# One product for values and denominators in an attention block followed by SwiGLU

## The chip, the cores and the metric

The kernel runs on one core of one Trainium2 chip. Its time is the device time of one execution in microseconds. Lower is better. The engines are named as in the profile: PE (matrix products), DVE (VectorE), ACT (ScalarE), POOL (GpSimd), SP (SyncE, which here only issues transfers).

## The reference

Attention over 4 batches, 8 heads, 768 positions and a head dimension of 64, with a mask and a bias, then a feed-forward block over the 3072 tokens of 512 features:

```
scores = q @ k.T / 8 - slope[h] * dist          # dist = 96 for far global keys
keep   = (key < 8) | (0 <= query - key < 96)    # 8 global keys, 96 local ones
a      = softmax(where(keep, scores, -1e9))
x      = a @ v                                   # to 3072 x 512
out    = (silu(x @ w_gate) * (x @ w_val)) @ w_out   # 512 -> 1536 -> 512
```

Inputs and the output are float32 in HBM.

## The kernel before

*Attention.* A batch has four pairs of heads (class `Pair`). Keys are cut into 7 chunks of 120, and each chunk is laid out with the 8 global keys in front, so that its 128 rows meet the 216 queries that can see it. Scores stand with keys on the partitions (`scores`, `scores_half`): the two heads of a pair use 64 rows of the array each. ACT takes the exponential into `at`, and DVE (POOL for some) multiplies it with a mask that holds the bias.

`values` (L386 to L439) forms one half of the queries (384) of one pair. With weights of 64 columns, head 0 writes partitions 0 to 63 and head 1 partitions 64 to 127: first a product with a tile of ones, which gives the denominator on all 64 partitions of a head (`den`), then a product with V (`num`). ACT copies the numerators to SBUF (`ns`, L419). DVE transposes the denominators in blocks of 32 by 32 (`dT`, L422), takes the reciprocal of 12 numbers a partition (`dR`, L423) and spreads it back by a second transpose (`rb`, L427). POOL, or DVE for batch 0, multiplies `ns` and `rb` into `xT` (L434), the input of the feed-forward part.

V stands in one tile for each batch, `vSs[b]`, of 128 x 7 chunks x 8 heads x 64 in float16. Its rows 8 and up are loaded by POOL, chunk by chunk (`load_v_rest`, L169), and its 8 global rows are copied from a small tile `vG` by SP (`copy_globals`, L183). POOL zeroes chunk 6 of batches 1 to 3 at the very start (L122); behind that in POOL's order stand the loads of v, and of k and q of heads 4 to 7, for the first half of batch 0, then weights, then the second half of k and q. For batch 0, V comes through a permutation by PE instead (`p_perm`, L547), with `v16` and `perm` as operands.

*Feed-forward.* Tokens go in 8 tiles of 384. For each tile and each of 12 column blocks f, `gate_or_val` makes a gate product and a value product of four matmuls each (`gps`, `vps`; L477), in a ring of three PSUM banks. ACT takes a tanh of the gate (`th`), and DVE makes `sl` (L490) and `hT` (L494) of it. `out_part` (L506) multiplies `hT` of the tile before with `wo`, three matmuls at a time. There are three buffers for `hT`.

*Order.* Everything stands in an order written out by hand. A prologue forms the first half of batch 0. Then seven stretches go through the tiles, and each has a list of attention steps that are strewn evenly between the feed-forward products (`stretches`, and the loop at L723; `quota` sets the spacing). The third stretch holds the first half of batch 1, the fourth (tiles 2 and 3) the second half of batch 1 and the first half of batch 2 (`both(1)`), the fifth (tiles 4 and 5) `both(2)`, the sixth (tile 6) the second half of batch 3. What a step leaves for DVE and POOL (masks, inversions, spreads, `spread_keys`) goes to a list `later`; one entry of it runs before each product, and all of it before the next step. Loads are tied to a tile and a block f by `at_step`. Keys and queries of batches 2 and 3 are transposed by DMA from SP (`transposes_dma`, L441), from rows that POOL loads. The lines that set the value steps and the V loads:

```python
        return [[sc(b, 0, 2), sc(b, 1, 2)], [sc(b, 2, 2), sc(b, 3, 2), fetch(0, 1)],
                [va(b, 0, 1), va(b, 1, 1)], [sp(0), va(b, 2, 1), va(b, 3, 1), sp(1)],
...
        items += [lambda b=b, c=c: load_v_rest(b, c) for c in range(NCH)]
```

The functions that the diff touches, with the line numbers of the profile:

Of the kernel before, what the change touches and what calls it, by code (L numbers as in the profile page):

```python
# [37 lines left out]
def kernel(  # L38
# [65 lines left out]
    k32 = sb2.tile([128, H // 2, J2 * D], FP32, name="k32", tag="kst")  # L104
    q16 = sb2.tile([128, 2, H, J2 * D], FP16, name="q16", tag="qst")
    k16 = sb2.tile([128, 2, H, J2 * D], FP16, name="k16", tag="kst")
    v16 = sb.tile([128, H, J2 * D], FP16, name="v16")
    for hp in range(2):
        for st, src in ((k32, k), (q32, q)):
            nc.sync.dma_start(  # L110
# [6 lines left out]
            out=dst, in_=src[0, h0:h1, TB * half:TB * half + TB, :].rearrange(  # L117
                "h (p j) d -> p h (j d)", p=128))

    vSs = [sb.tile([128, NCH, H, D], FP16, name=f"vS{b}") for b in range(B)]  # L120
    for b in range(1, B):
        nc.gpsimd.memset(vSs[b][:, 6, :, :], 0.0)  # L122
    load_half(v16, v, 0, 0, H)
    load_half(k16[:, 0, 4:8], k, 0, 4, 8)
    load_half(q16[:, 0, 4:8], q, 0, 4, 8)
# [3 lines left out]
    nc.vector.memset(ones, 1.0)  # L129

    NC0 = 4
    perm = sb.tile([128, J2, NC0, 128], FP16, name="perm")
    nc.vector.memset(perm.rearrange("p j c m -> p (j c m)").bitcast(mybir.dt.uint32), 0)
    kTs = [sb.tile([128, NCH * 128], FP16, name=f"kT{i}") for i in range(NP)]

# [33 lines left out]
    def load_v_rest(b, c):  # L169
        n = min(KC, S - KC * c)  # L170
        nc.gpsimd.dma_start(  # L171
            out=vSs[b][NG:NG + n, c, :, :],
            in_=v[b, :, KC * c:KC * c + n, :].rearrange("h p d -> p h d"))


# [5 lines left out]
            in_=v[:, :, 0:NG, :].rearrange("b h p d -> p (b h) d"))  # L181

    def copy_globals(b):  # L183
        c0 = 3 if b == 0 else 0
        nc.sync.dma_start(
            out=vSs[b][0:NG, c0:, :, :],
            in_=vG[:, b, :, :].unsqueeze(1).broadcast_to([NG, NCH - c0, H, D]))


    def stage_rows(b):  # L190
# [60 lines left out]
    class Pair:  # L251
# [134 lines left out]
        def values(self, half, nd, keep, mul_eng):  # L386
            b, hp = self.b, self.hp
            lo, hi_q = HALF[half]
            num, den = nd
            parts = []  # L390
            if b == 0:
                for which in range(2):
                    for c, col, q0, n in SCORES[half, which]:
                        parts.append((c, (half, which), col, q0 - lo, n))
            else:
                for c in range(NCH):
                    cb, col, q0, n = chunks[c]
                    a, z = max(q0, lo), min(q0 + n, hi_q)
                    if a < z:
                        parts.append((c, cb, col + a - q0, a - lo, z - a))  # L400
            for dst, ones_side in ((den, True), (num, False)):
                for i, (c, cb, col, o, n) in enumerate(parts):
                    vals = vS3 if (b, half, c) == (0, 0, 3) else vSs[b][:, c]
                    for hi in range(2):
                        r = slice(64 * hi, 64 * hi + 64)
                        nc.tensor.matmul(  # L406
                            dst[r, o:o + n],
                            lhsT=ones[:, 0:64] if ones_side else vals[:, 2 * hp + hi, :],
                            rhs=self.at[cb][:, hi, col:col + n],
                            start=(i == 0), stop=(i == len(parts) - 1),  # L410
                            skip_group_check=True)
            dT = sb2.tile([128, TB], FP32, name="dT", tag="dT")
            dR = sb2.tile([128, TB // 32], FP32, name="dR", tag="dR")
            rb = sb2.tile([128, TB], FP32, name="rb", tag="rb")
            dst = x_of(2 * b + half)[:, hp, :]
            src = num[:, 0:TB]
            if keep:
                src = sb2.tile([128, TB], FP32, name="ns", tag="ns")
                nc.scalar.copy(out=src, in_=num[:, 0:TB])  # L419

            def invert():
                nc.vector.transpose(dT, den[:, 0:TB])  # L422
                nc.vector.reciprocal(  # L423
                    out=dR, in_=dT.rearrange("p (n i) -> p n i", i=32)[:, :, 0])

            def spread():
                nc.vector.transpose(  # L427
                    rb.rearrange("p (n i) -> p n i", i=32),
                    dR.unsqueeze(2).broadcast_to([128, TB // 32, 32]))
                if mul_eng is nc.gpsimd:  # L430
                    scale_num()

            def scale_num():
                mul_eng.tensor_mul(dst, src, rb)  # L434

            later.append(invert)
            later.append(spread)
            if mul_eng is not nc.gpsimd:
                later.append(scale_num)  # L439

        def transposes_dma(self):  # L441
            b, hp = self.b, self.hp
# [23 lines left out]

    def products(t, f, which, c0, c1, dst=None):
        if f == 0 and which == 0 and c0 == 0:
            hTs[t] = sb2.tile([128, NFF, TB], FP16, name="hT", tag="hT", bufs=3)
        if c0 == 0:  # L470
            if dst is None:
                dst = single("gv"[which] + "ps", state["x"][gv.get("n", 0) % len(state["x"])])
                gv["n"] = gv.get("n", 0) + 1
            gv[f, which] = dst
        w = (wg, wv)[which]
        for c in range(c0, c1):
            nc.tensor.matmul(  # L477
                gv[f, which][:, 0:TB], lhsT=w[:, c, 128 * f:128 * f + 128],
                rhs=x_of(t)[:, c, :],
                start=(c == 0), stop=(c == NC - 1))  # L480
# [112 lines left out]
    for c in range(3, NCH):  # L593
        load_v_rest(0, c)
    load_w(3)
    for b in range(1, B):
        copy_globals(b)
    run_later(9)
    p_sc(2)
# [26 lines left out]

    def va(b, hp, half):
        def step():
            pairs[b, hp].values(half, banks("nd"), True,
                                nc.vector if b == 0 else nc.gpsimd)  # L630
        return step

    def tr(b, hp):
# [11 lines left out]
        return step  # L645

    def second(b):
        return [[sc(b, 0, 2), sc(b, 1, 2)], [sc(b, 2, 2), sc(b, 3, 2)],
                [va(b, 0, 1), va(b, 1, 1)], [va(b, 2, 1), va(b, 3, 1)]]

    def first(b):
        return [[tr(b, 0), tr(b, 1)],
# [5 lines left out]
    def both(b):  # L658
# [6 lines left out]
        def sp(hp):  # L665
            return lambda: later.append(pairs[n, hp].spread_keys)

        return [[sc(b, 0, 2), sc(b, 1, 2)], [sc(b, 2, 2), sc(b, 3, 2), fetch(0, 1)],
                [va(b, 0, 1), va(b, 1, 1)], [sp(0), va(b, 2, 1), va(b, 3, 1), sp(1)],
                [sc(n, 0, 0), sc(n, 0, 1), fetch(2, 3)], [sp(2), sc(n, 1, 0), sc(n, 1, 1)],  # L670
                [va(n, 0, 0), sc(n, 2, 0)], [sp(3), sc(n, 2, 1), va(n, 1, 0)],
                [sc(n, 3, 0), sc(n, 3, 1)], [va(n, 2, 0)], [va(n, 3, 0)]]

    half1 = [[trh(0)], [trh(1)], [sch(0, 0)], [sch(0, 1)], [trh(2)], [sch(1, 0)], [sch(1, 1)],
# [34 lines left out]
        at_step(0 if c < 2 else 1, (10 + c) % 12, lambda c=c: load_v_rest(1, c))  # L709
    for c in range(4, NCH):  # L710
        at_step(1, 2 * c - 1 if c < 6 else 10, lambda c=c: load_v_rest(1, c))
    for b, base, rate in ((2, 23, 2.0), (3, 43, 1.4)):
        items = [lambda b=b: stage_rows(b)]
        for hp in range(NP):
            for i in (1, 0):
                for hi in range(2):
                    items.append(lambda b=b, i=i, h=2 * hp + hi: load_rows(b, i, h))
        items += [lambda b=b, c=c: load_v_rest(b, c) for c in range(NCH)]
        for n, it in enumerate(items):
            at_step((base + int(n / rate)) // NFF, (base + int(n / rate)) % NFF, it)  # L720

    outs = [(t, i, part) for t in range(NT - 1) for i in range(3) for part in range(4)]
    for n, (tiles, steps) in enumerate(stretches):  # L723
# [3 lines left out]
                groups.append((0.05 if t == 0 and f < 2 else 1.0, t, f, which))  # L727
            groups += [(1.1, t, f, 2)] * n_out
        work = sum(g[0] for g in groups)
        quota = len(steps) / (work - (1.0, 0, 5.0, 3.0, 3.0, 4.5, 3.0)[n])  # L730
        owed = -0.1 if n == 0 else 0.4
        for w, t, f, which in groups:
            if which == 0:
# [55 lines left out]
```

## Time and profile before

| | |
|---|---|
| median of 9 runs | 263.65 us (263.19 to 264.51) |
| the profiled execution | 263.21 us, of which the span from first to last instruction is 261.2 |
| PE busy | 247.4 us, 95% of the span |
| DVE busy | 184.3 us, 71% |
| ACT busy | 134.6 us, 52% |
| POOL busy | 100.3 us, 38% |
| tile 0 begins, tile 2, tile 4, tile 6, tile 7 (first gate product) | 20.4, 82.1, 140.6, 197.7, 225.5 us |

A line of the timeline gives the start and the length in us, the engine, the line, what is written and read, how many instructions are merged, and in brackets the idle time before them and what ended it. A line of the chain gives start, length and what. A line of waits and groups gives busy time, mean duration and idle time. Matmuls overlap, so a run of them is longer than its share of PE by the latency of the last one.

### The profile page before, as it was taken

To read this page: it belongs to the slowest core of one execution; us is meant where nothing else is said; L and a number is where in the kernel's file an instruction comes from. 1 tells how busy PE (TensorE), PEld (TensorE's weight loads), DVE (VectorE), ACT (ScalarE), POOL (GpSimd) and SP (SyncE) were. 2 spreads that over 40 slices of the span, in tenths; PEclk is the share of its full clock that TensorE was granted. 3 is DMA by queue.
4 is the path that set the end of the run, shared out by engine and by line. 5 is a ranking of instruction groups with operands and counts; after the bars stand their busy time and mean duration, and the time that the engine had idled before them with its cause. 6 is when DMAs were issued, how large, how long until landed. Compare 5 with 4: busy or idle time off the path is not lost.

```text
span 261.2 us, 5568 instructions
## 1 busy us (share of the span) xinstructions
PE 247.4 (95%) x2144; PEld 140.5 (54%) x2144; DVE 184.3 (71%) x422; ACT 134.6 (52%) x296; POOL 100.3 (38%) x117
## 2 busy tenths in 40 slices
PE   7977999899999999899999999999999999999993
PEld 4554555465655566445555566455555565555541
DVE  7388689967787667987966668978876659655510
ACT  3565687469873554445633654555534633332321
POOL 9663653000237947901438886701111223300000
PEclk9999999999999999999999999999999999999999
DMA  7999999970354999991059996991011101101122
GB/s 167 184 192 167 189 204 203 193 47 4 52 71 61 121 143 133 176 141 36 9 71 89 141 172 65 134 140 42 2 40 44 40 3 40 40 3 40 40 83 80
DMA packets 81010, 24.82 MB, mean 95 GB/s; under 512 B 66832, under 2 KB 77912, under 8 KB 80984
## 3 DMA queue, kind: packets, MB, share of 16 engines
q0 software_dynamic: 63264, 13.83, 65.2%
q1 hardware_dynamic: 17720, 10.64, 18.3%
q8 instruction: 17, 0.28, 0.5%
q14 instruction: 9, 0.07, 0.1%
HBM read 28.63 MB, written 6.29 MB: 134 GB/s over the span
## 4 chain that ended last, share of the span: by engine, by line
PE 68%; DVE 13%; DMA 8%; ACT 4%; issue 3%; POOL 2%; POOLq 0%; DVEq 0%; ACTq 0%
PE ops L506 20%; PE vps L477 19%; PE gps L477 18%; DMA q<-in_q_dram 8%; PE nd L406 6%; PE sc L358 3%; DVE sl L490 3%; DVE hT L494 2%; DVE rb L427 2%; DVE dT L422 2%; ACT at L367 2%; PE trs L262 1%; ACT th L488 1%; DVE dR L423 1%; DVE xT L434 1%
## 5 line engine op out<-in xcount | busy, mean ns | idle before, releaser
L488 ACT ACTIVATE th<-gps 128x384 f32<-128x384 f32 x94 | 46.5, 494 | 67.1 <-PE gps L477 65.1
L490 DVE SCALAR_TENSOR_TENSOR sl<-th,gps 128x384 f32<-128x384 f32 x94 | 51.4, 547 | 40.0 <-ACT th L488 39.6
L477 PE MATMUL vps<-xT,wv 128*128 128x384 f16 x376 | 76.6, 326 | 2.0 <-DVE sl L490 1.6
L477 PE MATMUL gps<-xT,wg 128*128 128x384 f16 x376 | 77.0, 326 | 1.3 <-DVE hT L494 0.8
L506 PE MATMUL ops<-wo,hT 128*128 128x512 f16 x288 | 75.7, 380 | 0.0
L434 POOL TENSOR_TENSOR xT<-ns,rb 128x384 f16<-128x384 f32 x24 | 24.0, 999 | 96.0 <-DVE rb L427 92.0
L494 DVE TENSOR_TENSOR hT<-vps,sl 128x384 f16<-128x384 f32 x94 | 51.3, 546 | 6.9 <-PE vps L477 0.5
L477 PEld LDWEIGHTS <-wg 128*128 128x128 f16 x384 | 36.1, 98 | 34.7 <-issue 3.8
L477 PEld LDWEIGHTS <-wv 128*128 128x128 f16 x384 | 36.0, 98 | 28.5 <-issue 5.1
L506 PEld LDWEIGHTS <-hT 128*128 128x128 f16 x288 | 26.9, 98 | 24.9 <-issue 0.9
L367 ACT ACTIVATE at<-sc 128x432 f16<-128x432 f32 x72 | 33.0, 538 | 3.7 <-PE sc L358 3.7
L171 POOL DMA_DIRECT2D vS<-in_v_dram x25 | 22.1, 886 | 7.1 <-DMA wo<-in_moe_w_out_dram 4.9
L511 ACT ACTIVATE osb<-ops 128x512 f32<-128x512 f32 x24 | 14.4, 598 | 19.9 <-PE ops L506 19.9
L419 ACT COPY ns<-nd 128x384 f32<-128x384 f32 x28 | 13.4, 478 | 17.2 <-PE nd L406 16.4
L427 DVE STREAM_TRANSPOSE rb<-dR 128x384 f32<-128x384 f32 x32 | 18.1, 568 | 0.9
L378 DVE TENSOR_TENSOR at<-at,masks 128x864 f16<-128x864 f16 x20 | 14.4, 721 | 3.4 <-ACT at L367 3.2
L422 DVE STREAM_TRANSPOSE dT<-nd 128x384 f32<-128x384 f32 x28 | 16.0, 573 | 0.3 <-PE nd L406 0.3
L343 ACT ACTIVATE at<-sc 128x432 f16<-128x432 f32 (+2 forms) x32 | 11.9, 444 | 5.8 <-PE sc L335 5.8
L406 PEld LDWEIGHTS <-ones 128*64 128x64 f16 x288 | 10.9, 110 | 7.3 <-issue 6.8
L196 POOL DMA_DIRECT2D kst<-in_k_dram x16 | 13.7, 872 | 0.0
L196 POOL DMA_DIRECT2D qst<-in_q_dram x16 | 13.6, 865 | 0.0
L406 PE MATMUL nd<-at,ones 128*64 128x216 f16 (+6 forms) x256 | 13.2, 230 | 0.0
(77 smaller groups left out, 190.3 us busy)
## 6 DMA issues: line engine op xcount, KB each, us to landing
out_dram<-osb SPq DMA_DIRECT2D x24, 256.0 KB, 2.1
vS<-in_v_dram POOLq DMA_DIRECT2D x21, 120.0 KB, 6.6
wg<-in_moe_w_gate_dram POOLq DMA_DIRECT2D x6, 256.0 KB, 8.8
wv<-in_moe_w_val_dram POOLq DMA_DIRECT2D x6, 256.0 KB, 8.8
wo<-in_moe_w_out_dram POOLq DMA_DIRECT2D x3, 512.0 KB, 12.2
kst<-in_k_dram POOLq DMA_DIRECT2D x16, 96.0 KB, 4.4
qst<-in_q_dram POOLq DMA_DIRECT2D x16, 96.0 KB, 5.8
kst<-in_k_dram POOLq DMA_DIRECT2D x2, 384.0 KB, 14.9
```

The costliest lines, as they stand in the source:

```text
L171: nc.gpsimd.dma_start(out=vSs[b][NG:NG + n, c, :, :], in_=v[b, :, KC * c:KC * c + n, :].rearrange("h p d -> p h d"))
L196: nc.gpsimd.dma_start(out=st[:, h // 2, :, h % 2, :], in_=src[b, h].rearrange("(t p) d -> p t d", p=128))
L367: nc.scalar.activation(out=at[:, hi, :], in_=sc[hi][:, 0:BANK], func=AF.Exp, scale=scale)
L406: nc.tensor.matmul(dst[r, o:o + n], lhsT=ones[:, 0:64] if ones_side else vals[:, 2 * hp + hi, :], rhs=self.at[cb][:, hi, col:col + n], sta ...
L422: nc.vector.transpose(dT, den[:, 0:TB])
L427: nc.vector.transpose(rb.rearrange("p (n i) -> p n i", i=32), dR.unsqueeze(2).broadcast_to([128, TB // 32, 32]))
L434: mul_eng.tensor_mul(dst, src, rb)
L477: nc.tensor.matmul(gv[f, which][:, 0:TB], lhsT=w[:, c, 128 * f:128 * f + 128], rhs=x_of(t)[:, c, :], start=(c == 0), stop=(c == NC - 1))
L488: nc.scalar.activation(out=th, in_=dst[:, 0:TB], func=AF.Tanh, scale=0.5)
L490: nc.vector.scalar_tensor_tensor(out=sl, in0=th, scalar=1.0, in1=dst[:, 0:TB], op0=AluOp.add, op1=AluOp.mult)
L494: nc.vector.tensor_mul(hTs[t][:, f, :], dst[:, 0:TB], gv["sl"])
L506: nc.tensor.matmul(ops, lhsT=hTs[t][:, f, 128 * i:128 * i + 128], rhs=wo[:, f, :], start=(f == 0), stop=(f == NFF - 1))
```

## The change

Batches 1 to 3 get a V tile `vO` in which each head's 64 columns of V are followed by 64 columns of ones. Batches 1 and 3 share one. POOL writes the ones and the zeroes of chunk 6 at the start, for two tiles. Twenty value steps (second half of batch 1, all of batches 2 and 3) go through a new function, `values_full`: for each head by itself one product a chunk with 128 columns of weights, [V|1] for head 0 and [1|V] for head 1, into a PSUM bank of its own. So numerators and denominators of a head stand on opposite halves of the partitions. ACT copies each head's numerators, DVE inverts each head's denominators (two transposes of 64 partitions and two reciprocals in place of one of each), and the spread and POOL's product stay one. First halves of batches 0 and 1 and the second half of batch 0 keep `values`.

In the stretches each of these steps stands alone instead of in pairs, some change places with score steps, and the spacing changes. The V loads of batches 2 and 3 no longer follow the loads of k and q at their pace but have places and a pace of their own. The global rows are copied chunk by chunk for batches 1 and 2 (14 transfers), and for batch 3 in the middle of tile 4. `hT` gets two buffers instead of three, and `v16` and `perm` use one of them; `ns` gets four.

```diff
-    v16 = sb.tile([128, H, J2 * D], FP16, name="v16")
+    hT_pro = sb2.tile([128, NFF, TB], FP16, name="v16perm", tag="hT")
+    v16 = hT_pro[:, 0:4, :].rearrange("p f t -> p (f t)").rearrange("p (h e) -> p h e", h=H)
...
-    vSs = [sb.tile([128, NCH, H, D], FP16, name=f"vS{b}") for b in range(B)]
+    vSs = [sb.tile([128, NCH, H, D], FP16, name="vS0")]
+    vOs = [None]
     for b in range(1, B):
-        nc.gpsimd.memset(vSs[b][:, 6, :, :], 0.0)
+        if b < 3:
+            vOs.append(sb.tile([128, NCH, H, 2, D], FP16, name=f"vO{b}"))
+            nc.gpsimd.memset(vOs[b][:, :, :, 1, :], 1.0)
+            nc.gpsimd.memset(vOs[b][:, 6, :, 0, :], 0.0)
+        else:
+            vOs.append(vOs[b - 2])
+        vSs.append(vOs[b][:, :, :, 0, :])
     load_half(v16, v, 0, 0, H)
...
-        c0 = 3 if b == 0 else 0
-        nc.sync.dma_start(
-            out=vSs[b][0:NG, c0:, :, :],
-            in_=vG[:, b, :, :].unsqueeze(1).broadcast_to([NG, NCH - c0, H, D]))
+        if b == 0:
+            nc.sync.dma_start(
+                out=vSs[b][0:NG, 3:, :, :],
+                in_=vG[:, b, :, :].unsqueeze(1).broadcast_to([NG, NCH - 3, H, D]))
+        else:
+            for c in range(NCH):
+                nc.sync.dma_start(out=vSs[b][0:NG, c], in_=vG[:, b])
...
+        def values_full(self, half, pv):
...
+            rows = (slice(0, 64), slice(64, 128))
+            for hi in range(2):
+                for i, (c, cb, col, o, n) in enumerate(parts):
+                    w0 = 4 * D * hp + D * hi
+                    nc.tensor.matmul(
+                        pv[hi][:, o:o + n],
+                        lhsT=vOs[b][:, c].rearrange("p h s d -> p (h s d)")[:, w0:w0 + 2 * D],
+                        rhs=self.at[cb][:, hi, col:col + n],
+                        start=(i == 0), stop=(i == len(parts) - 1),
+                        skip_group_check=True)
+                nc.scalar.copy(out=ns[rows[hi], :], in_=pv[hi][rows[hi], 0:TB])
+
+            def invert(hi):
+                r = rows[1 - hi]
+                nc.vector.transpose(dT[r, :], pv[hi][r, 0:TB])
+                nc.vector.reciprocal(
+                    out=dR[rows[hi], :],
+                    in_=dT[r, :].rearrange("p (n i) -> p n i", i=32)[:, :, 0])
...
+            for hi in range(2):
+                later.append(lambda hi=hi: invert(hi))
+            later.append(spread)
...
-            hTs[t] = sb2.tile([128, NFF, TB], FP16, name="hT", tag="hT", bufs=3)
+            hTs[t] = sb2.tile([128, NFF, TB], FP16, name="hT", tag="hT", bufs=2)
...
-        return [[sc(b, 0, 2), sc(b, 1, 2)], [sc(b, 2, 2), sc(b, 3, 2), fetch(0, 1)],
-                [va(b, 0, 1), va(b, 1, 1)], [sp(0), va(b, 2, 1), va(b, 3, 1), sp(1)],
+        return [[sc(b, 0, 2), sc(b, 1, 2)], [va(b, 0, 1)],
+                [sc(b, 2, 2), sc(b, 3, 2), fetch(0, 1)], [va(b, 1, 1)], [va(b, 2, 1)],
+                [sp(0), va(b, 3, 1), sp(1)],
                 [sc(n, 0, 0), sc(n, 0, 1), fetch(2, 3)], [sp(2), sc(n, 1, 0), sc(n, 1, 1)],
-                [va(n, 0, 0), sc(n, 2, 0)], [sp(3), sc(n, 2, 1), va(n, 1, 0)],
+                [va(n, 0, 0)], [sc(n, 2, 0), sc(n, 2, 1)], [sp(3), va(n, 1, 0)],
                 [sc(n, 3, 0), sc(n, 3, 1)], [va(n, 2, 0)], [va(n, 3, 0)]]
...
-    for b, base, rate in ((2, 23, 2.0), (3, 43, 1.4)):
+    for b, base, rate, v_base, v_rate in ((2, 23, 2.0, 31, 0.9), (3, 43, 1.4, 55, 0.8)):
...
+        items += [(v_base + c / v_rate, lambda b=b, c=c: load_v_rest(b, c)) for c in range(NCH)]
+        if b == 3:
+            items.append((v_base, lambda: copy_globals(3)))
...
-        quota = len(steps) / (work - (1.0, 0, 5.0, 3.0, 3.0, 4.5, 3.0)[n])
+        quota = len(steps) / (work - (1.0, 0, 5.0, 5.0, 5.0, 5, 3.0)[n])
```

## The prediction

> **What bounds the kernel now.** I read the engine shares first, then the chain that ended last, then windows by stage.
>
> ```profile
> PE 247.4 (95%) x2144; PEld 140.5 (54%) x2144; DVE 184.3 (71%) x422; ACT 134.6 (52%) x296; POOL 100.3 (38%) x117
> DMA  7999999970354999991059996991011101101122
> ```
>
> PE is the bound; DVE is second. The DMA engines are full from the second slice to the eighth (6.5 to 52 us). The chain's beginning and some value steps (the second and third block are the chain asked for by window):
>
> ```profile
> 0.74 1.45 POOL vS L122 x3
> 2.18 1.03 POOL v L116
> 12.90 13.61 DMA q<-in_q_dram
> 26.91 0.76 PE vps L477 x4
> ...
> 99.61 0.65 PE vps L477 x4
> 100.26 1.36 PE nd L406 x40
> 101.62 0.75 PE ops L506 x3
> ...
> 117.06 0.66 PE nd L406 x16
> 117.72 0.29 PE sc L358 x4
> 118.01 0.76 PE gps L477 x4
> ...
> 132.09 0.66 PE nd L406 x16
> 132.75 0.76 PE vps L477 x4
> ```
>
> Two things are to be seen. The chain opens with POOL: zeroing, then the loads that POOL issues. And a feed-forward product of four matmuls costs 0.65 us, but 0.76 after a run of half-array matmuls. So a double value step costs PE 1.36+0.10=1.46 us, a single one 0.66+0.11=0.77, one with half a score pair 0.66+0.29+0.11=1.06.
>
> The timeline of the start, and a later stall:
>
> ```profile
> 2.13 1.09 POOL L116 DMA_DIRECT2D v<-in_v_dram  x1
> 9.65 1.46 PE L550 MATMUL psv<-v,perm 128*128 128x512 f16 x6 [0.44 <-DMA v<-in_v_dram]
> 13.79 0.70 PE L324 MATMUL sc<-consts,slopeI 128*128 128x432 f16 x6
> 26.55 0.36 PE L288 MATMUL trs<-consts,q 128*64 128x128 f16 x6 [0.73 <-DMA q<-in_q_dram]
> 106.86 1.27 DVE L454 COPY kT<-kN 128x720 f16<-128x720 f16 x1
> 109.61 0.81 PE L477 MATMUL gps<-xT,wg 128*128 128x384 f16 x4 [0.81 <-DVE hT L494]
> ```
>
> PE waits for v at 9.65 and for the second half of q at 26.55: up to there both the DMA stream and the order on PE carry the time. Windows of tiles 2+3, 4+5 and of the first 9.35 us (columns: length, then PE, PEld, DVE, ACT, POOL busy, clock, DMA share, GB/s):
>
> ```profile
> 82.12:140.60 58.48, 56.96 (x465) 31.80 (x464) 45.48 (x101) 29.21 (x62) 31.27 (x36) 1.00 1.19 104
> 140.60:197.74 57.14, 56.63 (x465) 31.82 (x464) 43.59 (x98) 29.20 (x62) 26.80 (x29) 1.00 0.99 89
> 0.00:9.35 9.35, 7.30 (x66) 4.90 (x67) 6.01 (x32) 4.18 (x10) 7.99 (x15) 1.00 0.97 171
> ```
>
> **The change, part by part.**
>
> *Products.* Twenty value steps change (batch 1 second half, batches 2 and 3). Before, a pair's two heads ran side by side on two halves of the array: 600 columns (first half) or 696 (second), once for the ones and once for V. At 0.65 us for 1536 columns (0.423 ns each) that is 0.51 or 0.59 us of streaming. The full-array form runs the heads one after the other, once each: again 1200 or 1392 columns. So streaming is not saved; what goes is the change of array form around each run and the halved shortest matmuls. New cost: 0.51 and 0.59 us plus about 0.01 to 0.02 for each of the two shortest products, 0.545 and 0.60. That short full-array matmuls do not cost much more is in the L324 group: six with 1200 columns and six weight loads in 0.70 us, of which the last one's 0.17 is its own latency.
>
> Sum on PE: 12 second-half steps were six doubles, 6x1.46=8.8, and become 12x0.60=7.2; four single first-half steps 4x0.77=3.1 become 2.2; four with half a score pair 4x1.06=4.2 become 2.2+1.2. In all -3.3 us, on the bounding engine. Uncertainty 0.3, if the weights load as in the L324 group.
>
> The Trainium skill ("TensorE: Matmul & The Clock Gate", section "LDWEIGHTS (loading the stationary operand)") speaks against this: it gives a weight load as its number of columns over 1.2, so an estimated 107 ns for 128 columns, which the shorter products here would not cover. By it the steps would cost 8x0.107=0.86 and 10x0.107=1.07 us, 8.1 us more in all than my sum, and the prediction would be 272.6; the L324 group stands against it.
>
> *Zeroing and ones on POOL.* Three memsets of 512 elements (1.45 us) become two of 3584 (ones, in runs of 64) and two of 512, in front of the v, k and q loads in POOL's order. The two DVE memsets of 256 and 768 words took 0.272 and 0.698 us: 0.83 ns an element and 0.06 fixed, which gives 0.485 for 512 elements, as POOL shows (0.48). So 3.04 each, 7.05 in all, +5.6. Bounds: all 0.098 us of the one-element memsets fixed, +5.1; nothing fixed, +6.3. The runs of 64 are not in the trace; I take them as free and leave slower ones to the range.
>
> What of the 5.6 reaches PE? v is issued at 7.8 instead of 2.13. The quickest POOL load (120 KB on idle DMA engines) landed in 3.4 us; v has 384 KB, 264 more at 190 GB/s, so 4.8: it lands near 12.6 instead of 9.6, when it took 7.5 beside the SP loads. That is +3.0 for the order on PE. For the stream: in the first 9.35 us 171 GB/s moved 1.60 MB, of which SP's loads are 0.97. DMA was idle for 1.5 us after the issue at 69.1, so POOL's share starts at about 9.3, and the other 0.63 MB at 183 GB/s are late by 3.4 us. The second half of q lands 3.4 later, and PE, in order, too. From 50 us on PE almost never waits for a load, so nothing gives this back: **+3.4**, bounds +2.4 (v as quick as the shortest flight allows) and +6.3 (all of the slowest memsets). SP's 15 small copies of the global rows (14 of them with 128-byte pieces, against 3 large ones) at 0.69 us of issue end long before SP's first output at 64 us; bytes are about equal. The seven copies for batch 3 come near tile 4 on SP ahead of four transposes, about 5 us of issue, inside a span in which SP is idle for 11.
>
> *DVE and ACT.* A step's inversion becomes two, on 64 partitions each. The trace has no such shape; DVE's copies go by the elements of a partition (0.169 us for 56, 0.545 for 720), so I take each at the full 0.573+0.228; the lower bound is half of that, no change. DVE: +0.8 to 0.86 a step, 17 us in all. In tiles 2+3 and 4+5 eight steps each: 45.5+6.6=52 of about 57 us, and 43.6+6.6=50 of 56: 90%. ACT gets a second 0.48 copy a step, at half load. Each inversion sits in DVE's order ahead of a gate's `sl` or a value's `hT`, on which PE's three banks depend two products later. Laid out with pitches of 0.46 (sl, hT), 0.86 (inversion), 0.5 (spread), a value step alone ends with 0.2 to 0.3 us to spare; spread_keys and masks beside it do not always fit. In 82 to 250 us PE now stalls 3.8 us in feed-forward, 1.3 of it after the spread_keys copy that took 1.27 instead of 0.34 us while POOL ran. V loads spread out can remove some of that, and single steps end earlier before tile 7 (0.4). Against it the denser DVE: I take about 1 us in each of the two long stretches and -1.2 for what goes: **+0.8**, bounds -1.5 and +4.5. If DVE's cover goes, the next thing late is xT at the tile boundaries, then the transposed keys of pairs 2 and 3, which took 6 to 7 us to land and now have about 8 from the copy that frees their buffer.
>
> *V loads, buffers.* The loads of batches 2 and 3 have the same issues (0.9 us of POOL each), earlier and farther apart; chunk 3 lands at least 3 us before its step by their median 6.6 us: nothing. Two hT buffers instead of three: tile t's output products end before tile t+2 writes: nothing. Batch 3 shares batch 1's V tile; batch 1's last value step is over 40 us earlier: nothing. v16 and perm in an hT buffer add no wait.
>
> **Sum.** 263.2 (the profiled execution: span 261.2 and 2.0 around it) +3.4 -3.3 +0.8 = 264.1. The median of the runs is 0.4 above this execution: **264.5**.
>
> **Rivals.**
> 1. *Faster: DVE stays covered.* Start +3.0, PE -3.5, stalls -1.3 (the 1.3 us at 106 to 110 go and none comes): 263.65-1.8=261.9. For it: DVE waits 9.4 and 9.6 us for `th` in the two long stretches, which is room. It decides if start and stalls together stay under 2.8. Chance 0.27.
> 2. *DVE becomes the bound* in tiles 2 to 5: stalls +4.5, 268.2. For it: 90% and in-order waits. Against: five to six groups between steps let it recover. 0.17.
> 3. *Clock.* The L324 group took 1.22 us at 3.73 and 0.70 at 13.79: PE began at half rate. Its last matmul ended near 257.2 and the clock fell near 261.2, so 4 us of idleness close it. Between the last fill (9.2, perhaps 8.3 now) and v at 12.6 there are 3.4 to 4.3. If it closes, 4 us at half rate cost 2, less the 0.7 that PE then need not wait for q: 265.8. 0.10.
> 4. *The product saves nothing:* each weight load at its row's 98 ns bounds the shorter products: steps of 0.78 and 0.98, +6.5: 271.0. The L324 group speaks against it. 0.04.
>
> **Numbers.** The forecast keeps 0.42, spread over 263.2 to 266; about 0.53 us (0.2%) is what a measurement of this kernel can tell from no change, so of it 0.16 is "same" and 0.26 slower. With rival 1 mostly faster: faster 0.25, same 0.18, slower 0.57. Range 261.8 to 268.3; the likeliest case's own is 263.2 to 266.
>
> **What would show it.** v's issue on POOL near 7.8 and PE's first psv near 12.6; tile 0 some 3.4 us later; vps after a value step 0.65 and the pv runs 0.54 to 0.60; DVE near 90% in tiles 2 to 5; stalls of gps and vps for `hT` and `sl` there between 3 and 6 us. Wrong if ones in runs of 64 take much longer than 3 us, if half-height transposes take half the time, or if the weights of pv are not hidden.

## The result and the profile after

The changed kernel takes **266.08 us** (median of ten runs, 265.79 to 266.55) against 263.65 (31 runs beside it, 263.09 to 264.61): a ratio of 1.0093, 95% interval 1.0082 to 1.0105. It is slower by about 2.4 us. The forecast was 264.5 in a range of 261.8 to 268.3. The sign and the range held, the likeliest case's own range (263.2 to 266) was missed by 0.1. The profiled execution took 265.96 us, of which the span is 264.2: 3.0 more than the span of the kernel before.

First the engine shares and the DMA row of the page of the changed kernel:

```profile
PE 246.0 (93%) x1960; PEld 141.4 (54%) x1960; DVE 202.6 (77%) x462; ACT 144.5 (55%) x316; POOL 106.4 (40%) x118
DMA  5599999990136999996196999992011011101122
```

PE is busy for 1.4 us less in a span that is 3.0 longer: waiting was added, not work. DVE got 18.3 us, where the prediction had counted 17. The DMA row has a second slice that is half empty, as long as POOL writes ones and issues nothing.

The chain of the changed kernel, asked for over the first 30 us (start, length, what):

```profile
0.74 3.08 POOL vO L127
3.82 0.64 POOL vO L128
4.46 3.21 POOL vO L127
7.66 0.64 POOL vO L128
8.30 1.05 POOL v16perm L117
...
17.34 12.68 DMA q<-in_q_dram
```

The same place of the kernel before read "0.74 1.45", "2.18 1.03" and "12.90 13.61 DMA q". The second half of q now lands at 30.0 us instead of 26.5, 3.5 later.

The waits of PE in the stretch from 82 to 250 us, first of the kernel before and then of the changed one (total us, times, longest):

```profile
PE vps L477 <- DVE sl L490: 0.9, 3, 0.4
PE gps L477 <- DVE hT L494: 0.8, 1, 0.8
PE gps L477 <- POOL xT L434: 0.4, 2, 0.2
```

```profile
PE gps L534 <- POOL xT L492: 2.3, 3, 0.9
PE sc L371 <- DVE dT L483: 2.0, 4, 0.7
PE gps L534 <- POOL xT L447: 0.3, 1, 0.3
```

The old waits for `sl` and `hT` are gone. In their place PE waits at the first product of a tile for `xT`, and inside score runs for the bank whose denominators DVE has not yet transposed (`dT`). The view counts only idle time. Measured from where the feed-forward product ahead of it should be through (0.65 us after its start) to the start of the next one, four score runs take 1.57 or 1.08 us instead of 0.58. The timeline of the changed kernel shows such a run:

```profile
109.97 0.59 DVE L483 STREAM_TRANSPOSE dT<-pv 64x384 f32<-64x384 f32 x1
...
110.59 0.22 DVE L484 RECIPROCAL dR<-dT 64x12 f32<-64x12 f32 x1
110.73 0.45 PE L371 MATMUL sc<-qT,kT 64*128 64x216 f16 x5
110.83 0.56 DVE L551 TENSOR_TENSOR hT<-vps,sl 128x384 f16<-128x384 f32 x1
...
111.30 0.56 DVE L483 STREAM_TRANSPOSE dT<-pv 64x384 f32<-64x384 f32 x1
...
111.92 0.35 PE L371 MATMUL sc<-qT,kT 64*128 64x216 f16 x3 [0.74 <-DVE dT L483]
```

The second head's transpose stands behind `hT` in DVE's order, 1.3 us after the first head's, and the score run that PE has begun needs that bank.

With the starts of the tiles (20.4, 82.1 and 225.5 us became 24.6, 85.6 and 228.2 for tiles 0, 2 and 7), the change of the span divides as follows:

| | predicted | in the two profiles |
|---|---|---|
| start, up to the first product of tile 2 | +3.4 | +3.5 |
| value products on PE | -3.3 | -3.0 (from 15.9 to 12.9) |
| stalls of PE, 82 to 250 us | +0.8 | +2.7 (from 3.8 to 6.5) |
| sum | +0.9 | +3.2 (the span: +3.0) |

The stalls are here all time between two feed-forward products beyond the pitch of the first, and what the score runs take beyond 0.58 us. The value products are the runs of `nd` or `pv` between feed-forward products, with the scores that stood in one run with them before and stand alone now. Two terms were right within 0.3 us, and the third was too small by 2 us. The -0.2 us between the sum and the span lies in small differences of the pitches and at the end. So the stalls are nearly the whole miss: the prediction put the profiled execution at 264.1, and it took 265.96.

### The profile page after: what moved, and what is told of

It reads as the page before. It is cut to its first block, busy times and chain, and to the rows that moved or that the text cites. A ratio compares the mean times of both kernels' runs of the same rounds, so it can differ in the third digit from the quotient of the medians.

```text
span 264.2 us, 5286 instructions
## 1 busy us (share of the span) xinstructions
PE 246.0 (93%) x1960; PEld 141.4 (54%) x1960; DVE 202.6 (77%) x462; ACT 144.5 (55%) x316; POOL 106.4 (40%) x118
## 4 chain that ended last, share of the span: by engine, by line
PE 61%; DVE 16%; DMA 7%; POOL 6%; ACT 4%; issue 3%; POOLq 0%; DVEq 0%; ACTq 0%
PE ops L563 19%; PE vps L534 18%; PE gps L534 16%; DMA q<-in_q_dram 7%; DVE sl L547 3%; DVE dT L483 3%; PE pv L473 3%; DVE hT L551 3%; PE sc L371 3%; POOL vO L127 2%; ACT at L380 2%; DVE rb L489 1%; PE trs L275 1%; DVE dR L484 1%; DVE dT L435 1%
## 5 line engine op out<-in xcount | busy, mean ns | idle before, releaser
L547 DVE SCALAR_TENSOR_TENSOR sl<-th,gps 128x384 f32<-128x384 f32 x94 | 51.1, 544 | 24.2 <-ACT th L545 23.4
L534 PEld LDWEIGHTS <-wg 128*128 128x128 f16 x384 | 35.4, 97 | 31.3 <-issue 2.0
L479 ACT COPY ns<-pv 64x384 f32<-64x384 f32 x40 | 18.9, 472 | 13.5 <-PE pv L473 11.9
L483 DVE STREAM_TRANSPOSE dT<-pv 64x384 f32<-64x384 f32 x40 | 23.1, 577 | 1.9 <-ACT ns L479 1.3
L181 POOL DMA_DIRECT2D vO<-in_v_dram x21 | 18.8, 897 | 5.5 <-DMA wo<-in_moe_w_out_dram 4.9
L473 PEld LDWEIGHTS <-vO 128*128 128x128 f16 x184 | 13.7, 97 | 4.0
L391 DVE TENSOR_TENSOR at<-at,masks 128x864 f16<-128x864 f16 x20 | 13.0, 652 | 3.1 <-ACT at L380 2.9
L473 PE MATMUL pv<-at,vO 128*128 128x216 f16 (+6 forms) x184 | 14.8, 225 | 0.0
```

The source lines that it names most:

```text
L181: nc.gpsimd.dma_start(out=vSs[b][NG:NG + n, c], in_=v[b, :, KC * c:KC * c + n, :].rearrange("h p d -> p h d"))
L473: nc.tensor.matmul(pv[hi][:, o:o + n], lhsT=vOs[b][:, c].rearrange("p h s d -> p (h s d)")[:, w0:w0 + 2 * D], rhs=self.at[cb][:, hi, col:c ...
L479: nc.scalar.copy(out=ns[rows[hi], :], in_=pv[hi][rows[hi], 0:TB])
L483: nc.vector.transpose(dT[r, :], pv[hi][r, 0:TB])
L534: nc.tensor.matmul(gv[f, which][:, 0:TB], lhsT=w[:, c, 128 * f:128 * f + 128], rhs=x_of(t)[:, c, :], start=(c == 0), stop=(c == NC - 1))
L547: nc.vector.scalar_tensor_tensor(out=sl, in0=th, scalar=1.0, in1=dst[:, 0:TB], op0=AluOp.add, op1=AluOp.mult)
```

## The experiments

Theory A: the start costs what POOL's memsets in front of v's load take, the products gain 3 us, and the second inversion on DVE takes that back. Rival theories: the start is lost for another reason (R1); the added stalls come from PSUM banks that are held for DVE, not from DVE's load (R2); they come from the new order of steps or the V loads (R3). All ratios are against the kernel before, run on the same chip beside each.

| run | us | ratio, 95% interval |
|---|---|---|
| the change | 266.08 | 1.0082 to 1.0105 |
| e1 ones late | 263.24 | 0.9955 to 1.0004 |
| e2 before, with the memsets | 267.86 | 1.0132 to 1.0198 |
| e3 one inversion | 260.59 | 0.9857 to 0.9908 |
| e4 ACT copies denominators | 270.81 | 1.0241 to 1.0299 |
| e5 second head from a fixed tile | 265.84 | 1.0069 to 1.0107 |
| e6 paired steps | 281.76 | 1.0678 to 1.0730 |
| e7 one inversion, old V schedule | 261.25 | 0.9894 to 0.9931 |
| e8 ACT copies, inversion deferred | 258.81 | 0.9810 to 0.9884 |
| e9 one inversion, paired steps | 270.04 | 1.0174 to 1.0256 |
| e10 as e8, V of batch 2 earlier | 258.87 | 0.9755 to 0.9852 |
| e11 as e10, without the empty slot | 261.00 | 0.9848 to 0.9930 |
| e12 as e10, start as before | **257.47** | 0.9734 to 0.9804 |

**The start.** e1 writes the ones in tile 1, long before a value step reads them, and leaves the rest:

```diff
-            nc.gpsimd.memset(vOs[b][:, :, :, 1, :], 1.0)
...
+    def ones_of(b):
+        for c in range(NCH):
+            nc.gpsimd.memset(vOs[b][:, c, :, 1, :], 1.0)
...
+    at_step(1, 2, lambda: ones_of(1))
+    at_step(1, 3, lambda: ones_of(2))
```

> The changed kernel with the ones of both V tiles written by POOL in tile 1, in pieces of one chunk (448 elements, 0.43 us by the memset's rate), instead of at the start. Theory (the ones hold back the v, k and q loads, and that alone costs the start): tile 2 begins near 82.1 us as before the change instead of 85.6, and the time falls by 3.5 to 262.6. Rival (the start is late for the 14 small copies on SP and the shared buffer): tile 2 still begins after 84.5 and the time stays above 265. If the pieces lock DVE out in tile 1, up to 0.5 us of the gain is lost.

e2 puts memsets of as many elements into the kernel before, ahead of v's load, into weight tiles that are loaded later:

```diff
+    for t in (wo.rearrange("p f d -> p (f d)"), wv.rearrange("p c f -> p (c f)")):
+        t = t.rearrange("p (r s d) -> p r s d", s=2, d=D)
+        nc.gpsimd.memset(t[:, :, 1, :], 1.0)
+        nc.gpsimd.memset(t[:, 0:4, 0, :], 1.0)
     load_half(v16, v, 0, 0, H)
```

> The kernel before, with 6656 more elements of memset on POOL in front of its v load (values written into weight tiles that are loaded later; the result is the reference's). Theory: v is issued near 8.2 us, DVE's float16 copies wait for POOL, tile 0 begins 4 us later and tile 2 about 3.5 us later; 267.1 us. Rival (the transfers catch up, the loss came from elsewhere): tile 2 begins within 1 us of 82.1 and the time is under 264.7.

Measured: e1 263.24, 2.8 below the change, with the first product of tile 2 at 82.6 us (82.1 before, 85.6 in the change). e2 267.86, 4.1 above the kernel before on its chip (263.8). One takes 2.8 to 3.1 us off and the other puts 4.1 on by the memsets alone, so the start is theirs and R1 falls. Neither hit its figure: e1 had been put at 262.6, or up to 0.5 more, and e2 at 267.1. What e2 lost beyond the 3.5 us of the change is not settled; its profile, taken of its slowest execution (269.93 us), shows PE waiting 1.75 us for the second half of q and the granted clock at 0.50 from 33 to 36 us. From tile 2 on, e1 stalls exactly as the change does (score runs of 1.57 and 1.08 us, `xT` waits of 0.5 to 1.0), so these have nothing to do with the start.

**The second inversion.** e3 leaves out the second head's transpose; head 1 is divided by head 0's denominators:

```diff
-                nc.vector.transpose(dT[r, :], pv[hi][r, 0:TB])
+                r = rows[1]
+                if hi == 0:
+                    nc.vector.transpose(dT[r, :], pv[hi][r, 0:TB])
```

> The changed kernel without the second transpose of denominators: head 1 of each of the twenty steps is divided by the denominators of head 0, so that part of the computation is left out. It takes 20 transposes of 0.58 us off DVE and lets the second bank go with ACT's copy. Theory (DVE's second inversion makes banks and xT late in tiles 2 to 7): 1.5 to 2.5 us of the score and xT waits go, 263.6 to 264.6. Rival (the waits come from the order of the steps): under 0.5 us goes, 265.6 or more.

Measured: 260.59, 5.5 below the change and 3.1 below the kernel before, with the late start still in it. All score runs are back at 0.58 us, and of the stalls (6.5 us in the change, 3.8 in the kernel before) 1.4 are left. The waits of PE from 82 to 250 us in e3:

```profile
PE gps L536 <- POOL xT L447: 0.3, 1, 0.3
```

Of the 5.5 us, 5.1 are these stalls, and the rest lies in the start, where e3 changes nothing. So one transpose of 0.58 us, twenty times, costs about 5 us on PE, a little under half of the DVE time that it takes (11.5). That is more than was expected of this run, and more than the price by which rival 2 of the prediction stood (4.5).

**Bank or load?** e5 keeps DVE's work as it is, but lets the second head's transpose read a constant tile in SBUF. The bank is then free once ACT has copied the values:

```diff
+    fixed = sb.tile([128, TB], FP32, name="fixed")
+    nc.vector.memset(fixed, 1000.0)
...
-                nc.vector.transpose(dT[r, :], pv[hi][r, 0:TB])
+                nc.vector.transpose(dT[r, :], (fixed if hi else pv[0])[r, 0:TB])
```

> The changed kernel, but the second head's transpose of denominators reads a constant tile in SBUF instead of the head's PSUM bank (so the second head is divided by a fixed number; its denominators are left out). DVE has the same number of instructions of the same shapes, and the bank of the second head is free as soon as ACT has copied the values. Theory that the banks held for DVE's queue make the stalls: the long score runs (1.58 and 1.09 us in place of 0.58, together 3.0 us in the stretch 82 to 250) fall to 0.58, the waits for xT at the tile boundaries (3.3 us) stay; time 263 to 263.6. Theory that it is DVE's load, whatever the bank: DVE stays late by as much, and PE waits as long for something else; time 265.5 to 266.5.

Measured: 265.84, as the change. All score runs take 0.58 us, as R2 wanted, but the time does not move. The waits of PE from 82 to 250 us in e5:

```profile
PE gps L537 <- POOL xT L495: 2.4, 3, 1.0
PE vps L537 <- DVE sl L550: 1.3, 2, 0.6
PE gps L537 <- POOL xT L450: 0.3, 1, 0.3
```

The waits for `dT` became waits for `sl`, and the stalls are 6.4 us, as in the change (6.5). The bank is only where the lateness shows; DVE's order is what is late. R2 falls.

**Order and loads.** e6 is the change with the order of steps and the spacing of the kernel before:

```diff
-        return [[sc(b, 0, 2), sc(b, 1, 2)], [va(b, 0, 1)],
-                [sc(b, 2, 2), sc(b, 3, 2), fetch(0, 1)], [va(b, 1, 1)], [va(b, 2, 1)],
-                [sp(0), va(b, 3, 1), sp(1)],
+        return [[sc(b, 0, 2), sc(b, 1, 2)], [sc(b, 2, 2), sc(b, 3, 2), fetch(0, 1)],
+                [va(b, 0, 1), va(b, 1, 1)], [sp(0), va(b, 2, 1), va(b, 3, 1), sp(1)],
...
-        quota = len(steps) / (work - (1.0, 0, 5.0, 5.0, 5.0, 5, 3.0)[n])
+        quota = len(steps) / (work - (1.0, 0, 5.0, 3.0, 3.0, 4.5, 3.0)[n])
```

> The changed kernel with the order of steps of the kernel before: two value steps in one place, and the number of groups between places of before. Four inversions then stand together in DVE's order. If single steps are what keeps DVE's cover, the time goes up by 2 to 4 us, to 268 to 270, with waits for hT and sl after each double step. If the order does not matter and only DVE's total counts, 265.5 to 266.5. If the order was a part of the loss (a value step directly ahead of scores and of tile boundaries), 264 to 265.

Measured: 281.76, far beyond all three expectations. The waits of PE from 82 to 250 us in e6:

```profile
PE sc L371 <- DVE dT L483: 5.2, 6, 1.3
PE gps L534 <- POOL xT L492: 4.9, 3, 2.9
PE vps L534 <- DVE sl L547: 2.9, 5, 1.0
```

Part of the loss is the clock, which comes below. e9 takes the same paired order with one inversion only (head 1 divided by head 0's denominators, as in e3):

> The changed kernel with one inversion a step (the second head's denominators are left out, 260.59 us with single steps) and the order of steps of the kernel before, two value steps in one place. DVE then has no more work than in the kernel before, in the order of before; only the products and the start are new. If the single steps are what made the run with one inversion 3 us quicker than start and products alone explain, this gives 263.5 to 265 (before 263.65, start +3.5, products about -3). If the order is worth nothing while DVE has room, 260.3 to 261.3.

Measured: 270.04, 9.5 above e3, with the clock at full rate throughout. DVE's work per step is then nearly that of the kernel before (one short reciprocal more), and it waits longer for ACT's `th` than in e3 (19.1 against 15.6 us). The timeline of e9 shows where it goes wrong:

```profile
108.54 0.23 DVE L486 RECIPROCAL dR<-dT 64x12 f32<-64x12 f32 x1
...
109.27 0.57 DVE L491 STREAM_TRANSPOSE rb<-dR 128x384 f32<-128x384 f32 x1
109.31 0.36 PE L371 MATMUL sc<-qT,kT 64*128 64x216 f16 x4
...
109.87 0.59 DVE L485 STREAM_TRANSPOSE dT<-pv 64x384 f32<-64x384 f32 x1
...
110.52 0.36 PE L371 MATMUL sc<-qT,kT 64*128 64x216 f16 x4 [0.85 <-DVE dT L485]
```

A value step of the new form leaves three entries in `later`, the old one two, and one entry goes ahead of each product. Two steps together leave six; at 109.3 us PE has come to the next step, and DVE has the second pair's transpose still ahead of it. So the single steps, with their spacing, are what the new form needs: without them it loses 9.5 us with one inversion (e9) and 15.7 with two (e6). That the *number of entries*, apart from their length, is the cause is read from this timeline and was not tried by itself.

e7 gives the kernel of e3 the old rates of the V loads (same omission):

```diff
-    for b, base, rate, v_base, v_rate in ((2, 23, 2.0, 31, 0.9), (3, 43, 1.4, 55, 0.8)):
+    for b, base, rate, v_base, v_rate in ((2, 23, 2.0, 31, 2.0), (3, 43, 1.4, 55, 1.4)):
```

> The changed kernel with one inversion a step (the second head's denominators are left out, as in the run with one inversion, 260.59 us) and the V loads of batches 2 and 3 at the rates of before (2.0 and 1.4 a group in place of 0.9 and 0.8). With one inversion the stretch from tile 2 on stalls about 3 us less than before's. If spreading the loads is what removed before's stall at 106 to 110 us (POOL beside DVE's spread copy), 1 to 1.5 us come back: 261.6 to 262.1. If the single steps removed it, nothing changes: 260.3 to 260.9.

Measured: 261.25, 0.66 above e3, on another chip and with intervals that touch (0.9894 to 0.9931 against 0.9857 to 0.9908). The spread-out loads are worth something between nothing and 1 us; what else shortened the stalls of the kernel before from 3.8 us to e3's 1.4 is not settled.

**Taking the second inversion away without leaving it out.** e4 lets ACT copy both heads' denominators into one SBUF tile, so that DVE inverts both at once:

```diff
                 nc.scalar.copy(out=ns[rows[hi], :], in_=pv[hi][rows[hi], 0:TB])
+                nc.scalar.copy(out=dn[rows[hi], :], in_=pv[hi][rows[1 - hi], 0:TB])
...
+                nc.vector.transpose(dT, dn)
```

> The changed kernel with ACT copying each head's denominators to SBUF too, side by side on 128 partitions, so that DVE inverts once a step as before the change and the banks are released by ACT alone. ACT gets 40 more copies of 0.47 us. Theory (DVE's load and the late release): score waits for dT (3.0 us) go and the xT waits (3.3 us) fall by half or more, less some lateness of the tanh behind ACT's copies: 262.5 to 264. Rival (ACT becomes the late one): 266 or more, with gps and vps waiting for sl that waits for th.

Measured: 270.81, a clear miss. DVE is down to its old load and yet PE waits more. The waits of DVE and of PE in e4, over the whole run:

```profile
DVE dT L484 <- ACT dn L481: 22.1, 16, 2.1
```

```profile
PE vps L533 <- DVE sl L546: 8.1, 16, 0.8
```

Sixteen times DVE stands at the transpose for up to 2.1 us, since ACT has four copies of 0.47 us to make, and the next gate's tanh stands behind them. The load is smaller, but the order now has a wait at its head. e8 moves things by one or two entries: denominators first, an empty entry, then the inversion, and the numerators' copies behind the tanh. It also takes the ones to tile 1 as e1 does and lets DVE write the zeroes:

```diff
+            later.append(lambda: None)
+            later.append(lambda: (keep(0), invert()))
+            later.append(lambda: keep(1))
             later.append(spread)
```

Here `keep(hi)` is ACT's copy of a head's numerators.

> A whole kernel: ones written at tile 1, zeros by DVE at the start, ACT copies both heads' denominators first and the numerators two and three groups later, and DVE inverts both heads at once from SBUF, two groups after the products. If the loss of the run with ACT copies (270.8) came from DVE blocking in order on ACT's copy and from the tanh queued behind four copies, the deferral removes it: DVE 69%, no waits for xT over 0.2 us, score runs 0.58; start as with the late ones (2.8 us sooner than in the change): 257.5 to 259.5. If ACT's extra 0.47 us copies are themselves what is late (tanh behind them), it stays above 262.

Measured: 258.81, inside the expected 257.5 to 259.5. DVE's waits for `dn` fell from 22.1 us to 0.4, and ACT at 63% carries the copies unseen. e10 loads the V of batch 2 a little faster, and e11 besides that drops the empty entry, so that a copy of numerators stands ahead of the tanh:

```diff
-    for b, base, rate, v_base, v_rate in ((2, 23, 2.0, 31, 0.9), (3, 43, 1.4, 55, 0.8)):
+    for b, base, rate, v_base, v_rate in ((2, 23, 2.0, 31, 1.2), (3, 43, 1.4, 55, 0.8)):
```

```diff
-            later.append(lambda: None)
-            later.append(lambda: (keep(0), invert()))
-            later.append(lambda: keep(1))
+            later.append(lambda: keep(0))
+            later.append(lambda: (keep(1), invert()))
             later.append(spread)
```

> The kernel with ACT's copies of the denominators and the deferred inversion (258.81 us), with the V loads of batch 2 at 1.2 a group in place of 0.9. There one run of products waited 0.38 us for a V chunk at 116 us; if that is all that the loads cost, 258.3 to 258.6, and at most the 0.5 us of the earlier study's rate come back as a stall (259.3).

> As the run before it, but without the empty slot: the first head's numerators are copied ahead of the first group after the products, the inversion comes one group after them, the spread two groups after. The waits for xT at the tile boundaries (0.45 us, three times) get shorter by up to 1.2 us in all: 257.2 to 258.2. If a copy ahead of the tanh makes sl late, PE waits 0.2 to 0.4 us at each of the 20 steps instead and the time is 261 or more.

Measured: e10 258.87, no difference that can be told. e11 261.00: the earlier inversion lost 2 us (the stalls of PE from 82 to 250 us are 3.9 us, against 1.8 in e10). In the timeline of e11, ahead of tile 4, the value product behind a gate product starts at 135.75, but the gate's tanh stands behind ACT's copy, and everything on DVE behind the tanh:

```profile
136.01 0.47 ACT L482 COPY ns<-pv 64x384 f32<-64x384 f32 x1
136.38 0.48 ACT L546 ACTIVATE th<-gps 128x384 f32<-128x384 f32 x1
...
136.90 0.55 DVE L548 SCALAR_TENSOR_TENSOR sl<-th,gps 128x384 f32<-128x384 f32 x1 [1.65 <-ACT th L546]
```

In e8, whose order of ACT e10 shares, the same value product starts at 135.52, and the tanh stands ahead of the copies:

```profile
135.78 0.49 ACT L547 ACTIVATE th<-gps 128x384 f32<-128x384 f32 x1
...
136.17 0.94 ACT L482 COPY ns<-pv 64x384 f32<-64x384 f32 x2
...
136.30 0.55 DVE L549 SCALAR_TENSOR_TENSOR sl<-th,gps 128x384 f32<-128x384 f32 x1 [1.07 <-ACT th L547]
```

The 0.4 us that the tanh loses reach `dT`, `rb` and `xT`, and the three tile boundaries wait 0.8 us each instead of 0.45. That accounts for 1.1 of the 2 us; five waits of 0.1 to 0.25 us between 107 and 217 us make up the rest.

**A start like that of before.** In e8 and e10 v is issued at 1.26 us, earlier than ever, and tile 0 still begins at 22.2 and 24.2 us in their profiles, against 20.4 before. In e12 POOL has three memsets of 512 elements in front of v's load again (two of zeroes and the ones of one chunk):

```diff
             nc.gpsimd.memset(vOs[b][:, 6, :, 0, :], 0.0)
+            if b == 1:
+                nc.gpsimd.memset(vOs[b][:, 0, :, 1, :], 1.0)
```

> The kernel with deferred inversion and V loads of batch 2 at 1.2 a group (258.87 us), with the three memsets of 512 elements that the kernel before had ahead of v's load (two of zeros and one of ones) back on POOL, so that v is issued near 2.2 us as in the kernel before and not at 1.26. In the two profiles with v at 1.26 the first half of q came to PE at 6.48 and 7.71 us, and tile 0 began at 22.2 and 24.2 in place of 20.4. If v's early transfer is what held q back, tile 0 begins near 20.4 to 21 and the time is 256.6 to 257.8. If the start simply scatters by 2 us, it stays 258.2 to 259.5.

Measured: 257.47, ratio 0.9769 (0.9734 to 0.9804): 2.3% faster than the kernel before, and the quickest of this study. v is issued at 2.13 us and tile 2 begins at 82.67. Tile 0 begins at 21.89, so the theory that v's early transfer held q back is not shown by it: the time came where expected, the start only in part. The profile of e11, with v at 1.26 us too, begins tile 0 at 22.4, so e10's 24.2 is the odd one. From tile 2 on e12 stalls as e10 does (1.8 us), its interval overlaps e10's (0.9755 to 0.9852), and four of e10's six executions lie at 258.2 to 259.1 and two at 260.6 and 261.1. That e12's start is worth 1.4 us is therefore not shown; the gain over the kernel before is. The windows of tiles 2+3 and 4+5, of the change and of e12 (length, then PE, PEld, that is its weight loads, DVE, ACT, POOL busy, clock, DMA share, GB/s; the DMA column goes above 1 and is not used here):

```profile
85.63:142.65 57.02, 55.69 (x393) 31.86 (x392) 50.08 (x116) 33.32 (x70) 30.53 (x35) 1.00 1.14 108
142.65:200.17 57.52, 55.68 (x394) 31.94 (x393) 49.74 (x115) 33.31 (x70) 26.05 (x27) 1.00 0.82 88
```

```profile
82.67:138.04 55.37, 55.03 (x393) 31.92 (x392) 44.49 (x101) 39.96 (x86) 31.44 (x37) 1.00 1.37 112
138.04:193.37 55.33, 55.04 (x394) 31.92 (x393) 43.59 (x99) 39.96 (x86) 25.21 (x27) 1.00 0.86 91
```

DVE gives 6 us in each to ACT (33.3 to 40.0), and PE is left with 0.3 us of idle time where it had 1.3 and 1.8.

## Why the prediction was right, and where it was not

**Start, +3.4: right, for the stated reason.** v was issued at 8.25 us (predicted 7.8), the first `psv` came at 13.80 (predicted 12.6), and the memsets took 3.08 and 3.26 us (predicted 3.04). The second half of q was 3.5 us late and PE with it; e1 and e2 confirm that it is the memsets. Two things on the way were not in the forecast: DVE's copies stood still beside the memsets, and the granted clock fell (0.50 from 9.5 to 11 us). Rival 3 had the fall with 0.10, but from the wait for v; here it followed 3.63 us in which PE waited for DVE's cast of k. That its price, 265.8, lies near the measured 266.08 is chance, since tile 2 is late by no more than the 3.5 us of the start. Both happened before v landed, and the order on PE was later than forecast (`psv` and tile 0 by 4.2 us instead of 3.0 to 3.4); 0.65 us of that went into the wait for q that PE had anyway, so that neither shows at tile 2. The prediction knew of this slack (the 0.7 in rival 3), but the forecast had neither delay; that they stayed within it, with 0.08 us left, is luck.

**Products, -3.3: right.** The runs take 0.614 us (second half) and 0.548 (first half) from one feed-forward product to the next, predicted 0.60 and 0.545, and the value part as a whole is 3.0 us shorter. Rival 4 falls, and with it the estimate that was worked out from the Trainium skill ("TensorE: Matmul & The Clock Gate", section "LDWEIGHTS (loading the stationary operand)"): the rows last 97 ns, near the skill's 107, but ten of them belong to a run of 0.614 us, so they lie beside the products. What failed is the step from a load's length to a cost of its own.

```profile
L473 PEld LDWEIGHTS <-vO 128*128 128x128 f16 x184 | 13.7, 97 | 4.0
```

**Half-height transposes at full price: right.** They take 577 ns in the page's group of the changed kernel, 573 for the full height in the trace of before. One row behind the assumption was misread: the 0.545 us for copies of 720 elements is a mean of six at 0.34 and two at 1.06 and 1.27 us. The assumption held all the same:

```profile
L483 DVE STREAM_TRANSPOSE dT<-pv 64x384 f32<-64x384 f32 x40 | 23.1, 577 | 1.9 <-ACT ns L479 1.3
```

**Stalls, +0.8: the step that failed.** They grew by 2.7 us. The prediction had "about 1 us in each of the two long stretches and -1.2 for what goes". Both sides were too small: e3 puts the second inversion at 5.1 us of stall, and what went was 2.4 (from 3.8 to e3's 1.4). The share of DVE was judged well (90% predicted, 86 to 88% measured in the windows). The way from there to PE was not: the pitches that left "0.2 to 0.3 us to spare" for a value step alone looked only at `sl` and `hT`, on which PE's three banks depend. They left out the second head's bank, which the next score run needs, and the last value step of a tile, whose `xT` the next tile's first product needs. `xT` was named as "the next thing late" and costed at nothing: the waits at tile boundaries are 3.3 of the 6.5 us (0.7 before), and the banks in score runs 3.0 (nothing before). The prediction looked for 3 to 6 us, on `hT` and `sl`.

**Rivals.** Rival 1 (DVE stays covered) is false for the change, but it is what e12 is like. Rival 2 (DVE becomes the bound) is half true: its mechanism is the one that decides, at 2.7 of its 4.5 us, because of what the rest of the change takes off. The forecast between the two lay too near to rival 1.

**Costed at nothing:** ACT's added copies, two `hT` buffers and the V tile that two batches share show in no wait of PE. POOL's loads and the V schedule did no harm either; e7 leaves open that the schedule gained up to 1 us.

## What to carry to other kernels

When a second engine takes on work, don't ask only for its share of the time: list every tensor and every buffer that it hands on, in its order, and ask for each who needs it next; at 87% one more instruction of 0.58 us cost nearly half of its length on the engine that bounds. Moving the work elsewhere helps only if the receiving engine's queue is arranged too: the same copies cost 4.7 us in e4 and gained some 4 in e8 (7.3 less the 2.8 that the late ones are worth; e8 also moves the zeroes to DVE), by their place in the queues of ACT and DVE. And the order of steps seems to have to fit the number of entries that a step leaves behind (read from e9's timeline, not tried by itself); undoing the single steps and their spacing cost 15.7 us, some 5 of them through the clock.

## What the runs showed of the hardware

Beside POOL's memsets some copies of DVE stood still, in the changed kernel:

```profile
4.41 3.26 POOL L127 MEMSET vO<- 128x3584 f16 x1
...
4.55 3.27 DVE L154 COPY v16perm<-consts 128x160 f16<-128x160 f16 x1
```

The copy of 160 elements takes 3.27 us and ends 0.15 us after the memset, while such copies take 0.29 to 0.50 in e8, where POOL only issues loads; PE waits 3.63 us for DVE's next cast. The Trainium skill ("SBUF — State Buffer", section "Who interferes with whom") has it that VectorE in its fast two-port modes and GpSimd exclude each other for a whole instruction, and these rows agree as to the exclusion; which mode the copy ran in no run here shows.

The clock can fall without one long pause. In e6 PE ran only a few products between 110 and 113 us (0.54 us busy in two, 0.06 in the third), none of its gaps longer than 1.4 us, and then at half rate. The windows of PE in e6 (length, busy time, clock, DMA share, GB/s):

```profile
110.00:112.00 2.00, 0.54 (x5) 1.00 1.52 179
112.00:113.00 1.00, 0.06 (x2) 1.00 2.02 14
113.00:114.00 1.00, 1.00 (x5) 0.66 0.59 81
114.00:115.00 1.00, 1.00 (x4) 0.50 1.65 104
115.00:116.00 1.00, 1.00 (x4) 0.50 0.06 3
116.00:117.00 1.00, 1.00 (x5) 0.63 0.16 27
117.00:118.00 1.00, 1.00 (x7) 1.00 0.97 141
```

At 175 to 181.5 us the same happens for nearly 7 us. These 10 us at half rate are worth about 5 of the 15.7 that e6 lost against the change. In the same run a pause of 2.91 us, up to 244.85 us, left the clock at 1.00. So several shorter stalls close together did what one longer pause did not; how the busy time is counted, and from when, no run here varies.
